# Gated mix of attention and a memory-recurrent transformer, forward and backward: crossbar transposes placed elsewhere in the forward recurrence, the value product's halves reordered, backward weights issued by GpSimd, sweep buffers allocated earlier

## The chip, the cores and the metric

The kernel runs on one core of one Trainium2 chip. The metric is the time of one execution on the device in microseconds, the median of several runs. The profile is taken from one execution of its own. The core's engines are PE (matrix products; PEld is its weight load), DVE (VectorE), ACT (ScalarE), POOL (GpSimd) and SP (SyncE). SP and POOL also issue DMAs, each in its own order: what stands behind a DMA that waits on such a queue waits too.

## The reference: what is computed

The output is a gated mix of two blocks over the same input x (2048 tokens, 576 columns, bf16), and the kernel returns it with the gradients of all inputs and weights:

```python
g = sigmoid((x * gate_w).sum(-1, keepdims=True))
a = A(x)      # 32 heads of 18 columns, one common k and v for all heads, softmax over all 2048 tokens
b = B(x)      # see below
return g * a + (1 - g) * b        # then vjp with grad_out

# B: 64 segments of 32 tokens, 32 heads of 128 columns, memory of 8 rows
mem = mem0
for s in range(64):
    h = concatenate([mem, x[32*s : 32*s+32]])           # 40 rows
    q, k, v = h @ Wq, h @ Wk, h @ Wv
    o = softmax(mask(q k^T * scale)) v @ Wo
    mem = o[:8];  outs.append(o[8:])
```

B is a chain: a segment's memory is the output of the one before, so its small products can't be batched over segments. A's work is large and free of order.

## The kernel before

**Stages.** From the trace: preparation and A's q and dO products (0 to 186 us), q, k and v of B for those tokens that need no place in the chain (`b_proj`, to 512), the forward weave (512 to 2372), the bulk of B's attention of the tokens (`b_bulk`, to 3112), the backward weave (to 4850), the backward of the tokens, the weight gradients and the end of A (to 6235).

**The weave.** `weave` runs two generators by turns. In the forward weave one is `b_chain_fwd`: 64 segments, each cut into 16 pieces by its `yield`s. The other is `a_pass1`, A's first sweep: 64 blocks of 512 rows, each of 16 steps. After each piece of the chain one step of the sweep follows, two steps ahead at the start. Thus a segment of the chain takes as long as one block of the sweep, and the order of the instructions is what the two generators write down. Engines run their own queues in that order.

**A sweep step** (`a_pass1`) makes the scores of the next key tile (a_S, PE), their exponent (a_E, ACT, L1459), the products dP (a_dP, PE), their product with the exponent (a_W, two DVE instructions, L1489), and adds both to an accumulator (a_acc, PE). At the end of a block `a_post` (L1519) turns the accumulator and stores three results (otok, dqtok, sd); it starts by a crossbar transpose of the block's query tile from DRAM (a_qt, L1523), and it runs in the steps with n % 16 in (1, 2, 5).

**A chain segment** (`b_chain_fwd`, L277) makes q, k and v rows of 32 tokens and memory in the layout of four column groups (`proj`, through `proj_part`; four matmuls for each of five row tiles of the input, each 512 columns wide). k comes in pieces 1 to 4, q in 4 to 8. `load_k` (L301) is a crossbar transpose of the segment's key rows; it is called in piece 11 for the next segment. `stash` (L314) is a crossbar transpose of 128 columns of a B weight, whose result `stash_end` stores as st_WT for the backward pass; two are done per segment in segments 0 to 47: the first is issued in piece 7 and stored in piece 14, the second issued in piece 14 and stored at the head of the next segment. The rows made are stored by POOL (`rows_out`) and copied on from DRAM to DRAM by SP (`rows_copy`, L343). In piece 10 the scores go into the bank px (64 columns of memory scores, 64 of token scores; in piece 11 64 columns of denominators follow, tile name c_x), then an exponent c_E (ACT, L425). In piece 11 the denominators are inverted (c_rd, DVE, L432) and the probabilities c_pn are made (L434).

The value product has two halves of 512 columns. v0 is made in pieces 9 to 11 in c_pj; v1 in two quarters of 256 columns (`proj_cols`): the first quarter in the free half of the scores' bank px in pieces 11 and 12, the second in c_pj in piece 12. Pieces 13 to 16 make the output o, its store and the 32 heads' product with Wo in many small matmuls (`heads`).

**The projections and the sweep's buffers.** `b_proj` ends with stores of its tokens' rows (L233). The sweep's buffers (KV, VK, WK by `load_A_kv`, L1403; the query tiles a_QD) lie in pools that are opened after b_proj's pools are closed.

**The backward weave** runs `b_chain_bwd` (L842) against `a_pass2` (L1564), A's second sweep. Its weights are loaded at its start: `load_WT` (L836) with six DMAs of 128 x 32 x 288 elements, all on SP; `load_WoT` (L550) with five DMAs, by turns on SP and POOL (`dq_eng`). The sweep's tiles b_QD (L1576) and b_SD (L1578) also come by SP's queue.

Of the kernel before, what the change touches and what calls it, by code (L numbers as in the profile page):

```python
# [11 lines left out]
BF16 = mybir.dt.bfloat16  # L12
F32 = mybir.dt.float32
P = 128

D = 576
NKT = 5
# [8 lines left out]
NPR = 16  # L26
# [13 lines left out]
class Kern:  # L40
# [169 lines left out]
    px = {}  # L210
# [47 lines left out]

    def proj_cols(self, out, st, Wt, lo, n, kts):
        for kt in kts:  # L260
            for c in range(4):
                self.mm(out[32 * c:32 * c + 32, :], lhsT=st[:, kt, :], rhs=Wt[:, kt, c * 1024 + lo:c * 1024 + lo + n],
                        start=(kt == 0), stop=(kt == NKT - 1), tp=(0, 32 * c))

    def proj_mem(self, st, Wt, j, psum, tag, nb):
# [10 lines left out]
    def b_chain_fwd(self, keep, sp, psum):  # L276
        nc = self.nc  # L277
# [39 lines left out]
        def stash_end(t, c):  # L317
            nc.sync.dma_start(self.st_WT[c // HB][:, c % HB, :], t[:])
# [5 lines left out]

        kx, vx = load_k(0), load_v(0)
        hs = hx = None
        for s in range(NSEG):
# [39 lines left out]

            if 0 < s <= 48:
                stash_end(*wt)
            if s:  # L370
# [11 lines left out]
            yield  # L382
            proj("k", 0, (0,), "c_pj")
            yield
            proj("k", 0, (1, 2, 3), "c_pj")
            yield
            proj("k", 0, (4,), "c_pj")
# [6 lines left out]
            rows_out("k")  # L394
            proj("q", 0, (1, 2), "c_pj")
            yield
            proj("q", 0, (3, 4), "c_pj")
            proj("q", 1, (0,), "c_x")
            if s < 48:
                wt = stash(2 * s)  # L400
            yield
            proj("q", 1, (1, 2, 3, 4), "c_x")
            rows_copy("k")
# [4 lines left out]
            rows_out("q")  # L408
            proj("v", 0, (0, 1), "c_pj")
            yield  # L410
            px = psum.tile([P, 512], F32, name="c_x", bufs=1)
            ps, den = px[:, 0:P], px[:, P:192]
# [12 lines left out]
            nc.scalar.activation(Et[:].rearrange("p a b -> p (a b)"), ps, ACT.Exp, scale=SCALEB)  # L425
            proj("v", 0, (2, 3), "c_pj")
            yield
            proj("v", 0, (4,), "c_pj")
            self.mm(den, lhsT=self.blockones[:], rhs=Et[:, 0, :], start=True, stop=False)
# [7 lines left out]
            nc.gpsimd.dma_start(self.pm_dram[s], pn[:].rearrange("p a b -> p (a b)"))  # L437
            if not last:
                kx = load_k(s + 1)
            vlo = px[:, 256:512]  # L440
            self.proj_cols(vlo, h_, self.W["v"], 512, 256, (0, 1, 2))
            yield
            self.proj_cols(vlo, h_, self.W["v"], 512, 256, (3, 4))
            nc.scalar.copy(t2["v"][:, 4:6, :].rearrange("p u e -> p (u e)"), vlo)
            pv = psum.tile([P, 512], F32, name="c_pj", bufs=1)
            self.proj_cols(pv[:, 0:256], h_, self.W["v"], 768, 256, range(NKT))
            nc.vector.tensor_copy(t2["v"][:, 6:8, :].rearrange("p u e -> p (u e)"), pv[:, 0:256])
            rows_copy("q")
# [14 lines left out]
            if not last:  # L463
                vx = load_v(s + 1)
                if s < 48:
                    stash_end(*wt)
                    wt = stash(2 * s + 1)
                ph = psum.tile([P, 512], F32, name="c_pj", bufs=1)
                heads(0, 11)
# [80 lines left out]
    def load_WoT(self, pool):  # L550
        self.WoT = pool.tile([P, NKT, J], BF16, name="WoT")
        self.nc.vector.memset(self.WoT[64:128, 4, :], 0.0)
        for kt in range(NKT):
            rows = KT_ROWS[kt]
            self.dq_eng().dma_start(self.WoT[0:rows, kt, :], self.st_WoT[kt][0:rows, :])

# [279 lines left out]
    def load_WT(self):  # L836
        for hf in range(2):
            c = slice(288 * hf, 288 * hf + 288)
            for wi in (2, 0, 1):
                self.nc.sync.dma_start(self.WT[wi][:, :, c], self.st_WT[wi][:, :, c])  # L840

# [561 lines left out]
    def load_A_kv(self, keep):  # L1403
        nc = self.nc
        self.KV = keep.tile([P, self.T], BF16, name="l_KV")
        nc.sync.dma_start(self.KV[:], self.kv_dram[:, :])
        self.VK = keep.tile([P, self.NTT, 64], BF16, name="l_VK")
        nc.sync.dma_start(self.VK[:], self.vk_dram[0])
        self.WK = keep.tile([P, self.NTT, 64], BF16, name="l_WK")
        nc.sync.dma_start(self.WK[:], self.vk_dram[1])  # L1410

    def a_qd_all(self, sp, psum):
# [24 lines left out]
    def a_pass1(self, keep, sp, psum, xps):  # L1437
# [3 lines left out]
        dl_all = keep.tile([P, NTT, NPR, 2, 2], BF16, name="a_dl")  # L1441
        QD, S, E_, W_ = {}, {}, {}, {}

        def load(b):
            if b < NB:
                p, qb = b // 4, b % 4
                QD[b] = sp.tile([P, 512], BF16, name="a_QD", bufs=3)
                nc.sync.dma_start(QD[b][:], self.qd_dram[p][:, qb * 512:(qb + 1) * 512])

# [16 lines left out]

        load(0)
        load(1)
        mm_S(0)
        ex(0)  # L1470
# [3 lines left out]
        for n in range(NP_ + 1):  # L1474
            if n < NP_:
                kt = n % 16
                if kt == 11:
                    load(n // 16 + 2)
                if n + 1 < NP_:
                    mm_S(n + 1)  # L1480
                dP = [psum.tile([P, 512], F32, name="a_dP", bufs=3) for _ in range(2)]
                for i in range(2):
                    r = slice(64 + 32 * i, 96 + 32 * i)
                    self.mm(dP[i][:], lhsT=self.KV[r, kt * P:kt * P + P], rhs=QD[n // 16][r, :], tp=(64 + 32 * i, 0))
                if n + 1 < NP_:
                    ex(n + 1)
                W_[n] = sp.tile([P, 2, 512], BF16, name="a_W", bufs=2)
                for i in range(2):
                    nc.vector.tensor_tensor(out=W_[n][:, i, :], in0=dP[i][:], in1=E_[n][:, i, :], op=ALU.mult)  # L1489
            if n > 0:  # L1490
                if n % 16 == 1:
                    acc = psum.tile([P, 512], F32, name="a_acc", bufs=1)
                    acc_mm(acc, n - 1, E_, self.VK, True, False)
                acc_mm(acc, n - 1, W_, self.WK, False, n % 16 == 0)
                if n % 16 == 0:
                    acs = sp.tile([P, 512], F32, name="a_acs", bufs=1)
                    nc.scalar.copy(acs[:], acc[:])
                    bb = n // 16 - 1
                    QD.pop(bb)
                    post = self.a_post(bb // 4, bb % 4, acs, sp, xps, dl_all)  # L1500
            if n < NP_ and n % 16:
                acc_mm(acc, n, E_, self.VK, False, False)
            if post is not None and n % 16 in (1, 2, 5):
                if next(post, "end") == "end":
                    post = None
            yield
# [12 lines left out]
    def a_post(self, p, qb, acs, sp, psum, dl_all):  # L1519
        nc = self.nc  # L1520
        dq_ = nc.gpsimd if (p, qb) == (NPR - 1, self.T // 512 - 1) else nc.sync
        qt = sp.tile([P, 4, 4, 32], BF16, name="a_qt", bufs=1)
        nc.sync.dma_start_transpose(qt[:].rearrange("p a b c -> p a (b c)"), self.qd_dram[p][:, qb * 512:(qb + 1) * 512])  # L1523
        pt = psum.tile([P, 4, P], F32, name="c_x", bufs=1)
# [6 lines left out]
        ptf = pt[:].rearrange("p a b -> p (a b)")  # L1531
        nc.scalar.copy(tkf, ptf)
        yield
        rl = sp.tile([P, 4, 2, 2], F32, name="a_rl", bufs=2)
# [203 lines left out]
def build_full(tc, A_x, A_wq, A_wk, A_wv, A_wo, B_mem0, B_Wq, B_Wk, B_Wv, B_Wo, gate_w, grad_out, outs_raw,  # L1738
# [9 lines left out]
    with SB("const") as cpool, tc.tile_pool(name="dram", bufs=1, space=bass.MemoryType.DRAM) as dram:  # L1748
# [14 lines left out]
        with ExitStack() as man:  # L1763
            man.enter_context(tc.manual_schedule())
            with SB("bwo") as bwo, SB("bw1") as bw1:
# [10 lines left out]
                with SB("bw2") as bw2:  # L1776
                    k.alloc_W(bw2, ("q",))
                    with SB("pxs") as pxs, PS("pxp") as pxp:
                        def extra(n):
                            if n == n0:  # L1780
                                for kt in range(NKT):
                                    k.load_W("q", kt)
                        k.b_proj(items, n0, len(items), pxs, pxp, extra)
                    with SB("a2k") as a2k, SB("cfs") as cfs, PS("cfp") as cfp, SB("a2s") as a2s, PS("a2p") as a2p:
                        k.load_A_kv(a2k)
                        k.weave(k.b_chain_fwd(a2k, cfs, cfp), k.a_pass1(a2k, a2s, a2p, cfp), 2)
            with SB("xw") as xw, SB("xl") as xl, SB("xs") as xs, PS("xp") as xp:
# [89 lines left out]
```

## Time and profile before

| | us |
|---|---|
| median of 3 runs | 6238.07 (6232.29 to 6254.74) |
| profiled execution | 6236.93 |
| its span in the trace | 6234.9 |
| forward weave, 512 to 2372 | 1860 |
| bulk of B's attention, 2372 to 3112 | 740 |
| backward weave, 3112 to 4850 | 1738 |
| PE busy | 5645.8 (91% of the span) |
| DVE busy | 3794.9 (61%) |
| ACT busy | 3389.5 (54%) |
| POOL busy | 1955.4 (31%) |

The profiled execution lies 1.1 us under the median. A row of the waits reads: engine, tile and line, then what released it, then the total of the waits in us, how many, and the longest. "issue" as a releaser means that the engine waited for nothing that the profile shows. SPq is SP's DMA queue.

### The profile page before, as it was taken

To read this page: it belongs to the slowest core of one execution; us is meant where nothing else is said; L and a number is where in the kernel's file an instruction comes from. 1 tells how busy PE (TensorE), PEld (TensorE's weight loads), DVE (VectorE), ACT (ScalarE), POOL (GpSimd) and SP (SyncE) were. 2 spreads that over 40 slices of the span, in tenths; PEclk is the share of its full clock that TensorE was granted. 3 is DMA by queue.
4 is the path that set the end of the run, shared out by engine and by line. 5 is a ranking of instruction groups with operands and counts; after the bars stand their busy time and mean duration, and the time that the engine had idled before them with its cause. 6 is when DMAs were issued, how large, how long until landed. Compare 5 with 4: busy or idle time off the path is not lost.

```text
span 6234.9 us, 214080 instructions
## 1 busy us (share of the span) xinstructions
PE 5645.8 (91%) x91339; PEld 3294.1 (53%) x91550; DVE 3794.9 (61%) x7192; ACT 3389.5 (54%) x4852; POOL 1955.4 (31%) x3481
## 2 busy tenths in 40 slices
PE   6898999999999998999859999999999899899998
PEld 4443444444444445777725555555555687675444
DVE  4335877777787886666558888888887111111112
ACT  3325777777777775656547777777776222211101
POOL 3002333333333334444413333333333211112213
PEclk9999999999999999999969999999999899999999
DMA  4645666666666548999864344443434899896653
GB/s 144 217 154 118 129 128 121 126 123 130 128 129 118 114 98 224 255 255 251 249 176 108 108 108 108 109 110 109 110 110 102 212 250 251 232 278 202 219 184 110
DMA packets 1426721, 998.59 MB, mean 160 GB/s; under 512 B 965597, under 2 KB 1245030, under 8 KB 1415814
## 3 DMA queue, kind: packets, MB, share of 16 engines
q1 hardware_dynamic: 1344294, 790.82, 52.0%
q0 software_dynamic: 81472, 194.07, 9.9%
q8 instruction: 717, 11.75, 0.8%
q14 instruction: 238, 1.95, 0.1%
HBM read 550.31 MB, written 385.03 MB: 150 GB/s over the span
## 4 chain that ended last, share of the span: by engine, by line
PE 34%; ACT 11%; issue 9%; DMA 5%; SPq 2%; POOL 2%; DVE 0%; POOLq 0%; DVEq 0%; ACTq 0%
ACT b_E L1597 10%; PE w_acc L75 10%; PE b_S L75 6%; PE r_pj L75 4%; PE r_x L75 3%; DMA dsx_dram<-x_dS 3%; PE x_tr L80 2%; PE b_acc L75 2%; PE x_po L75 1%; PE x_b L75 1%; PE x_m L75 1%; PE f_big L75 1%; PE b_dP L75 1%; PE x_S L75 1%; SPq L840 1%
## 5 line engine op out<-in xcount | busy, mean ns | idle before, releaser
L1489 DVE TENSOR_TENSOR a_W<-a_dP,a_E 128x512 bf16<-128x512 f32 x2048 | 1318.4, 686 | 357.1 <-issue 135.7
L1618 DVE TENSOR_TENSOR b_dS<-b_dP,b_E 128x512 bf16<-128x512 f32 x2048 | 1312.9, 683 | 268.5 <-issue 149.6
L1459 ACT ACTIVATE a_E<-a_S 128x1024 bf16<-128x1024 f32 x1024 | 1048.2, 1024 | 472.1 <-PE a_dP L75 229.1
L1597 ACT ACTIVATE b_E<-b_S 128x1024 bf16<-128x1024 f32 x1024 | 1047.8, 1023 | 457.3 <-PE b_dP L75 358.5
L75 PE MATMUL b_S<-b_KV,b_QD 32*128 32x512 bf16 x2048 | 406.2, 386 | 192.7 <-ACT b_E L1597 117.8
L75 PE MATMUL r_pj<-WT,r_dT 128*32 128x288 bf16 x12288 | 493.6, 288 | 1.1 <-ACT r_hs L950 1.1
L75 PE MATMUL w_acc<-w_d,w_h 128*128 128x512 bf16 (+1 forms) x2352 | 470.9, 379 | 2.5
L75 PE MATMUL a_S<-a_QD,l_KV 32*128 32x512 bf16 x2048 | 402.2, 386 | 27.8 <-ACT a_E L1459 10.4
L75 PE MATMUL b_acc<-b_dS,b_SD 128*32 128x512 bf16 x2048 | 424.2, 396 | 1.5 <-DMA b_SD<-sd_dram 1.2
L75 PE MATMUL a_acc<-a_W,l_WK 128*32 128x512 bf16 x4096 | 417.5, 393 | 1.6 <-issue 1.3
L75 PE MATMUL a_acc<-a_E,l_VK 128*32 128x512 bf16 x4096 | 409.7, 384 | 6.6 <-issue 2.7
L75 PE MATMUL b_acc<-b_E,b_SD 128*32 128x512 bf16 x2048 | 409.0, 396 | 0.0
L75 PE MATMUL b_dP<-b_KV,b_QD 32*128 32x512 bf16 x2048 | 404.7, 391 | 1.3 <-DVE b_dS L1618 1.3
L75 PE MATMUL a_dP<-a_QD,l_KV 32*128 32x512 bf16 x2048 | 401.9, 388 | 3.5 <-issue 3.5
L75 PEld LDWEIGHTS <-r_dT 128*32 128x32 bf16 x12288 | 333.7, 97 | 80.4 <-issue 2.0
L1084 DVE COPY y_T<-y_pt 128x512 bf16<-128x512 bf16 x256 | 96.8, 419 | 451.1 <-PE y_pt L80 433.7
L75 PEld LDWEIGHTS <-b_QD 32*128 32x128 bf16 x4096 | 165.6, 91 | 389.1 <-issue 315.1
L75 PEld LDWEIGHTS <-w_h 128*128 128x128 bf16 (+1 forms) x2688 | 229.8, 100 | 258.4 <-issue 6.6
L75 PEld LDWEIGHTS <-hm 128*32 128x32 bf16 x8960 | 226.6, 97 | 238.1 <-issue 79.6
L75 PEld LDWEIGHTS <-l_KV 32*128 32x128 bf16 x4096 | 119.3, 91 | 321.0 <-issue 288.9
L1070 ACT CAST y_tdk<-y_pk 128x512 bf16<-128x512 f32 x128 | 75.0, 586 | 377.7 <-PE y_pk L75 213.4
L75 PE MATMUL y_pdx<-WT,y_T 128*128 128x288 bf16 x2048 | 271.8, 286 | 0.0
(422 smaller groups left out, 11253.6 us busy)
## 6 DMA issues: line engine op xcount, KB each, us to landing
b_QD<-qd_dram SPq DMA_DIRECT2D x256, 128.0 KB
b_SD<-sd_dram SPq DMA_DIRECT2D x256, 128.0 KB
dOx_dram<-p_tok SPq DMA_DIRECT2D x16, 1024.0 KB
c_vx<-vx_dram SPq DMA_DIRECT2D x256, 64.0 KB
krow_dram<-c_k POOLq DMA_DIRECT2D x64, 256.0 KB, 3.1
qrow_dram<-c_q POOLq DMA_DIRECT2D x64, 256.0 KB, 3.6
vrow_dram<-c_v POOLq DMA_DIRECT2D x64, 256.0 KB, 5.4
x_q<-qx_dram SPq DMA_DIRECT2D x32, 512.0 KB
```

What stands on the lines that cost most here:

```text
L75: return self.nc.tensor.matmul(out, lhsT, rhs, start=start, stop=stop, tile_position=tp, skip_group_check=True)
L80: return self.nc.tensor.transpose(out, in_, self.identB[b:b + nrows, b:b + nrows], tile_position=tp)
L840: self.nc.sync.dma_start(self.WT[wi][:, :, c], self.st_WT[wi][:, :, c])
L1070: nc.scalar.copy(d[w][:, r, :], pk[:])
L1084: nc.vector.tensor_copy(T_[t][w][:], pt[:])
L1459: nc.scalar.activation(E_[n][:], S.pop(n)[:], ACT.Exp, scale=SCALEA)
L1489: nc.vector.tensor_tensor(out=W_[n][:, i, :], in0=dP[i][:], in1=E_[n][:, i, :], op=ALU.mult)
L1597: nc.scalar.activation(E_[n][:], S.pop(n)[:], ACT.Exp, scale=SCALEA)
L1618: nc.vector.tensor_tensor(out=D_[n][:, i, :], in0=dP[i][:], in1=E_[n][:, i, :], op=ALU.mult)
```

## The change

It has four parts.

1. The order of the crossbar transposes in the forward weave. `load_k(s)` is called in piece 2 of the segment that uses it. `a_post` has one more `yield` and transposes a_qt after it, and runs in the steps (1, 2, 3, 6). `stash` is called in pieces 3 and 6, `stash_end` in 6 and 9.
2. The value product. v0 is made in pieces 8 to 10 and copied out in halves by ACT and DVE; v1 is made in c_pj in full width of 512 in pieces 11 and 12. px holds the scores and denominators alone. `proj_cols` is gone. One group of q's second half comes a piece earlier.
3. The DMAs of `load_WT` and `load_WoT` are all issued by GpSimd's queue.
4. The sweep's buffers and query tiles lie in a pool that is opened before the last projections, and their loads are issued four items before the end of those.

```diff
 # b_chain_fwd
-        kx, vx = load_k(0), load_v(0)
+        vx = load_v(0)
...
-            if 0 < s <= 48:
-                stash_end(*wt)
...
             proj("k", 0, (0,), "c_pj")
+            kx = load_k(s)
             yield
             proj("k", 0, (1, 2, 3), "c_pj")
+            if s < 48:
+                wt = stash(2 * s)
...
             proj("q", 0, (1, 2), "c_pj")
+            if s < 48:
+                stash_end(*wt)
+                wt = stash(2 * s + 1)
             yield
             proj("q", 0, (3, 4), "c_pj")
-            proj("q", 1, (0,), "c_x")
-            if s < 48:
-                wt = stash(2 * s)
-            yield
-            proj("q", 1, (1, 2, 3, 4), "c_x")
+            proj("q", 1, (0, 1), "c_x")
+            yield
+            proj("q", 1, (2, 3, 4), "c_x")
+            proj("v", 0, (0,), "c_pj")
             rows_copy("k")
...
-            proj("v", 0, (0, 1), "c_pj")
-            yield
-            px = psum.tile([P, 512], F32, name="c_x", bufs=1)
+            proj("v", 0, (1, 2), "c_pj")
+            if s < 48:
+                stash_end(*wt)
+            yield
+            px = psum.tile([P, 192], F32, name="c_x", bufs=1)
...
-            proj("v", 0, (2, 3), "c_pj")
-            yield
-            proj("v", 0, (4,), "c_pj")
+            self.proj_part(pj["v", 0], h_, self.W["v"], 0, (3, 4))
+            nc.scalar.copy(t2["v"][:, 0:2, :].rearrange("p u e -> p (u e)"), pj["v", 0][:, 0:256])
+            nc.vector.tensor_copy(t2["v"][:, 2:4, :].rearrange("p u e -> p (u e)"), pj["v", 0][:, 256:512])
+            yield
...
-            if not last:
-                kx = load_k(s + 1)
-            vlo = px[:, 256:512]
-            self.proj_cols(vlo, h_, self.W["v"], 512, 256, (0, 1, 2))
-            yield
-            self.proj_cols(vlo, h_, self.W["v"], 512, 256, (3, 4))
-            nc.scalar.copy(t2["v"][:, 4:6, :].rearrange("p u e -> p (u e)"), vlo)
-            pv = psum.tile([P, 512], F32, name="c_pj", bufs=1)
-            self.proj_cols(pv[:, 0:256], h_, self.W["v"], 768, 256, range(NKT))
-            nc.vector.tensor_copy(t2["v"][:, 6:8, :].rearrange("p u e -> p (u e)"), pv[:, 0:256])
+            proj("v", 1, (0, 1), "c_pj")
+            yield
+            proj("v", 1, (2, 3, 4), "c_pj")
             rows_copy("q")
...
                 vx = load_v(s + 1)
-                if s < 48:
-                    stash_end(*wt)
-                    wt = stash(2 * s + 1)
 # load_WoT
-            self.dq_eng().dma_start(self.WoT[0:rows, kt, :], self.st_WoT[kt][0:rows, :])
+            self.nc.gpsimd.dma_start(self.WoT[0:rows, kt, :], self.st_WoT[kt][0:rows, :])
 # load_WT
-                self.nc.sync.dma_start(self.WT[wi][:, :, c], self.st_WT[wi][:, :, c])
+                self.nc.gpsimd.dma_start(self.WT[wi][:, :, c], self.st_WT[wi][:, :, c])
 # load_A_kv (the same function load, with load(0) and load(1), is gone from a_pass1)
+                self.QD[b] = keep.tile([P, 512], BF16, name="a_QD", bufs=3)
+                nc.sync.dma_start(self.QD[b][:], self.qd_dram[p][:, qb * 512:(qb + 1) * 512])
...
+        load(0)
+        load(1)
 # a_pass1
-            if post is not None and n % 16 in (1, 2, 5):
+            if post is not None and n % 16 in (1, 2, 3, 6):
 # a_post
-        qt = sp.tile([P, 4, 4, 32], BF16, name="a_qt", bufs=1)
-        nc.sync.dma_start_transpose(qt[:].rearrange("p a b c -> p a (b c)"), self.qd_dram[p][:, qb * 512:(qb + 1) * 512])
...
         nc.scalar.copy(tkf, ptf)
+        yield
+        qt = sp.tile([P, 4, 4, 32], BF16, name="a_qt", bufs=1)
+        nc.sync.dma_start_transpose(qt[:].rearrange("p a b c -> p a (b c)"), self.qd_dram[p][:, qb * 512:(qb + 1) * 512])
         yield
 # build_full
+                    with SB("a2k") as a2k:
+                        with SB("pxs") as pxs, PS("pxp") as pxp:
...
+                                elif n == len(items) - 4:
+                                    k.load_A_kv(a2k)
-                    with SB("a2k") as a2k, SB("cfs") as cfs, PS("cfp") as cfp, SB("a2s") as a2s, PS("a2p") as a2p:
-                        k.load_A_kv(a2k)
-                        k.weave(k.b_chain_fwd(a2k, cfs, cfp), k.a_pass1(a2k, a2s, a2p, cfp), 2)
+                        with SB("cfs") as cfs, PS("cfp") as cfp, SB("a2s") as a2s, PS("a2p") as a2p:
+                            k.weave(k.b_chain_fwd(a2k, cfs, cfp), k.a_pass1(a2k, a2s, a2p, cfp), 2)
```

More of the change, by code (lines that the diff above doesn't have):

```diff
@@ L257, in proj_part @@
                         start=(kt == 0), stop=(kt == NKT - 1), tp=(0, 32 * c))
[L259 to L263, printed above, removed]
     def proj_mem(self, st, Wt, j, psum, tag, nb):
@@ L1410, in load_A_kv, with load @@
         nc.sync.dma_start(self.WK[:], self.vk_dram[1])
+        self.QD = {}
+        def load(b):
+            if b < NPR * (self.T // 512):
+                p, qb = b // 4, b % 4
+                self.QD[b] = keep.tile([P, 512], BF16, name="a_QD", bufs=3)
+                nc.sync.dma_start(self.QD[b][:], self.qd_dram[p][:, qb * 512:(qb + 1) * 512])
+        self.load_QD = load
+        load(0)
+        load(1)
     def a_qd_all(self, sp, psum):
@@ L1441, in a_pass1 @@
         dl_all = keep.tile([P, NTT, NPR, 2, 2], BF16, name="a_dl")
[L1442 to L1448, printed above, removed]
+        S, E_, W_ = {}, {}, {}
+        QD, load = self.QD, self.load_QD
         def mm_S(n):
@@ L1465, in acc_mm @@
                         rhs=t[:, g // 2, :], start=first, stop=last, tp=(0, 32 * g))
-        load(0)
-        load(1)
         mm_S(0)
@@ L1777, in build_full, with extra @@
                     k.alloc_W(bw2, ("q",))
[L1778 to L1783, printed above, removed]
-                    with SB("a2k") as a2k, SB("cfs") as cfs, PS("cfp") as cfp, SB("a2s") as a2s, PS("a2p") as a2p:
-                        k.load_A_kv(a2k)
-                        k.weave(k.b_chain_fwd(a2k, cfs, cfp), k.a_pass1(a2k, a2s, a2p, cfp), 2)
+                    with SB("a2k") as a2k:
+                        with SB("pxs") as pxs, PS("pxp") as pxp:
+                            def extra(n):
+                                if n == n0:
+                                    for kt in range(NKT):
+                                        k.load_W("q", kt)
+                                elif n == len(items) - 4:
+                                    k.load_A_kv(a2k)
+                            k.b_proj(items, n0, len(items), pxs, pxp, extra)
+                        with SB("cfs") as cfs, PS("cfp") as cfp, SB("a2s") as a2s, PS("a2p") as a2p:
+                            k.weave(k.b_chain_fwd(a2k, cfs, cfp), k.a_pass1(a2k, a2s, a2p, cfp), 2)
             with SB("xw") as xw, SB("xl") as xl, SB("xs") as xs, PS("xp") as xp:
```

## The prediction

> **What bounds the kernel now.** I read the page first, then the stages, the waits of each stage, and the timeline around the longest. The page has PE busy for 91% of the span, but it also gives DVE 61% and ACT 54%, so the loss must be looked for by stage. The row of the forward weave (stretch, length, then busy PE, PEld, DVE, ACT, POOL, granted clock, DMA share, GB/s):
>
> ```profile
> 516.00:2371.00 1855.00, 1710.48 (x36718) 782.15 (x36711) 1467.84 (x2683) 1339.18 (x1724) 692.99 (x1406) 0.99 0.63 121
> ```
>
> PE is busy 92% at full clock, so 144.5 us are idle there. The waits of that stretch (total, how many, longest):
>
> ```profile
> DVE a_W L1489 <- issue: 135.7, 313, 5.3
> ACT a_E L1459 <- issue: 102.1, 72, 4.6
> PE c_x L75 <- DVE c_rd L432: 65.4, 64, 2.2
> PE c_pj L75 <- issue: 26.5, 23, 4.1
> ```
>
> Two kinds of loss stand here. One is a true wait, once in each of the 64 segments: PE waits 1.02 us for the reciprocal c_rd. The other is "issue": an engine stands still though nothing visible holds it. The timeline of one segment shows both (start, duration, engine, operation, wait in brackets):
>
> ```profile
> 1502.27 1.22 SPq L1523 DMA_TRANSPOSE a_qt<-qd_dram  x1
> ...
> 1508.84 0.41 PE L75 MATMUL c_x<-c_qT,c_kmT 128*8 128x8 bf16 x30
> 1510.12 0.17 PE L75 MATMUL c_x<-c_qT,c_kmT 128*8 128x8 bf16 x2 [0.88 <-issue]
> 1511.20 1.29 DVE L1489 TENSOR_TENSOR a_W<-a_dP,a_E 128x512 bf16<-128x512 f32 x2 [1.58 <-ACT c_E L425]
> 1511.77 0.23 PE L75 MATMUL c_x<-c_E,blockones 128*128 128x64 bf16 x2
> 1512.41 0.55 DVE L432 RECIPROCAL c_rd<-c_x 128x64 f32<-128x64 f32 x1
> 1513.01 0.51 PE L75 MATMUL c_x<-Wv,hm 128*32 128x256 bf16 x12 [1.00 <-DVE c_rd L432]
> ```
>
> c_rd reads the bank into which PE wants to write the value product, so PE waits until it is done. And the score products, many small instructions, stop for 0.88 us soon after a crossbar transpose was issued.
>
> I tested the second kind over the whole stage. The first a_S products of successive steps give each piece's length; the medians of pieces 1 to 16 sum to 27.41 us. The mean segment is 29.24 in segments 1 to 47, which also transpose two weight columns each, and 28.00 after. Put against the transposes' flights (DMA records of 256-byte reads): outside pieces 2 to 9, 146 pieces with a transpose in flight for over half their length exceed the median by 0.29 us, 110 partly covered by 0.23, 120 without by 0.09. In pieces 2 to 9, which hold wide products (few instructions per us), the excess is 0.02 with or without. In the later segments, narrow pieces show 0.23 with a flight and 0.03 without. So the loss sits where a transpose meets many small instructions.
>
> At the stage's start and in the backward weave:
>
> ```profile
> 506.34 0.33 SPq L1406 DMA_DIRECT2D l_KV<-kv_dram  x1
> 511.82 0.61 PE L75 MATMUL a_S<-a_QD,l_KV 32*128 32x512 bf16 x2 [10.13 <-DMA a_QD<-qd_dram]
> ```
> ```profile
> 3147.86 37.30 SPq L840 DMA_DIRECT2D WT<-st_WT  x6
> 3185.26 7.04 SPq L1576 DMA_DIRECT2D b_QD<-qd_dram  x1
> ```
> ```profile
> PE b_S L75 <- DMA b_QD<-qd_dram: 48.2, 2, 40.2
> ```
>
> SP's queue issues six weight loads for 37.30 us, and the sweep's tile b_QD stands behind them: PE waits 40.2 us once (the other 8 are the stage's start). Between 3155 and 3195 PE is busy 0.90 us.
>
> **Part 1: transposes moved.** Per segment SP issues the same DMAs in another order: a_qt, the keys and both weight columns now stand at pieces 2, 3 and 6 and their stores at 6 and 9, before the row copies that they followed. Adding SP's issue times, I place three of the four flights in pieces 4 to 8 and the second weight column in 12 to 13. In segments 1 to 47 the narrow excess is 146 x 0.29 + 110 x 0.23 + 120 x 0.09 = 78.4 us. At the 0.03 of the later segments without a flight, 376 narrow pieces would keep 11, so 67 go; 27 later ones give 27 x 0.20 = 5. That is the best case, 72. The second column stays in narrow pieces, 48 x 0.3 = 15: I take **−57**. The least, with 0.09 as the floor: 146 x 0.20 + 110 x 0.14 = 45, less 20 if the second column's flight spreads: −25.
> The price could be on SP. It now issues for 20.3 us per segment and waits 9.0; the two waits for the weight columns' landings are 2.8 each (146.9 us in 52). 20.3 + 2 x 2.8 = 25.9 us fits under PE's segment of some 27.5. The keys, formerly fetched a segment ahead, are now issued at about 7 us and land 5.2 later, at some 12; piece 10 wants them at about 14. That cover is 2 us.
>
> The Trainium skill speaks against this term: its page "Runtime: NRT & Kernel Launch", section "Instruction fetch mechanics", says that instructions are streamed in 16 KiB blocks by DMA and that crossing a block is mostly hidden. If the "issue" stops are such fetches and are hidden, this part is worth nothing and the sum is that of the first rival below; the row of 0.29 against 0.09 us decides for me that they are not hidden while transposes fly.
>
> **Part 2: value halves.** The second half no longer uses the scores' bank: as 512-wide products it waits for c_rd no more, 65.4 us. Per segment 20 matmuls and 20 weight loads go; the streamed columns stay. What is late next is DVE. Around piece 11 it must do a_W (1.29 for two), c_rd 0.55 and c_pn 0.29 in one piece, 2.13 us, where PE's piece with two groups takes 0.92 + 2 x 0.21 plus 0.23 for the denominators, 1.58; the step after then waits for a_W. So piece 11 goes from a median 2.77 to about 2.13, and piece 7, with one more group, pays 0.2 at most: −0.5 per segment, x 64 = **−30**. Bounds: −65 if DVE catches up for nothing, −10 if the halved value copy, now on DVE and ACT between the same steps, delays them by another 0.3 us (two copies of 256 columns).
>
> **Part 3: sweep buffers apart.** The KV load is issued four items earlier in the projections. PE's last product ends at 501.69 and it waits 10.13 at 511.82. The order of the changed program still lets the first exponent wait for the projections' last stores (issued 502.33, landed about 506): −6 (between −4 and −9.5).
>
> **Part 4: backward weights by GpSimd.** SP is free of the 37.30 us, so b_QD no longer waits: up to 40.2 + 2.3 (a wait for another weight, WoT) + a few us behind = −46. The loads (2304 KB each) now run on POOL after its dmT store at about 3149. Behind them on POOL are the next dO-memory tiles, the expansions and the products' weights. At the pace of the SP issue (6.2 us each), or 7.4, all six have landed by 3193; the chain's first product wants its half at about 3172, when two have. POOL's own issue cost per DMA, from its rows:
>
> ```profile
> 523.86 1.18 POOL L296 DMA_DIRECT2D otok_dram<-zeros  x1
> 2394.79 1.85 POOL L199 DMA_DIRECT2D WoN<-in_B_Wo_dram  x2
> ```
>
> That is 1.18 for 2048 rows and 0.92 for 1024, so some 2 us for the 4096 rows of a WT load (estimate). WoT's 4.5 MB wholly on POOL gain 2.3 and may delay a later tile by as much. I take **−40**. If each load took 12 us, POOL would hold PE for some 18 to 20 of the 40: the bound −20.
>
> The same skill also has a rule here: "DMA: Bandwidth & Descriptors", section "Issuing engines are not separate DMA queues", says that another issuing engine saves only the sequencer's issue time, usually small beside the transfer. By it this term would be about nothing; the rows show 37.30 us of issue on SP with b_QD's issue right behind, so here it is not small.
>
> **Sum** against the profiled execution's 6236.93: −57 − 30 − 6 − 40 = −133, 6104. The median of the runs is 6238.07, 1.1 more: **6105**.
>
> **Rivals.** (a) The issue stops are not the transposes'. For it: ACT a_E and DVE a_W wait for "issue" in all segments, and 0.09 remains without a flight. Against: 0.23 to 0.29 with. Then −76 remains: 6162. (b) GpSimd's loads are slow, at 12 us each: −113, 6125. For it: nothing of this size goes over that queue in this stage now. (c) SP becomes the bound. If its 25.9 us rise to 28.5 (one more landing wait of 2.6), segments 0 to 47 gain 29.24 − 28.5 = 0.74 each, 35 in all; with 40 + 6 and 8 from the last 16 segments that is −89: 6149. (d) DVE does not limit: the full 65 gives −168: 6070. (e) **Slower**: SP falls into a row of landing waits. Its queue is in order, and each transposition's store waits for the transposition, with key rows and value loads behind. The gains elsewhere (40 + 6 + 8 = 54) over 48 segments are 1.1 us, so it decides from 29.24 + 1.1 = 30.4 us per segment. At 31.5 (20.3 + 9.0, and 2.2 of the row copies' mean wait once more) it costs 48 x 2.26 = 108, less 54: 6292. (f) It does less than it says: at 30 us per segment, 37 lost and 54 won, −17: 6221.
>
> **Chances.** Forecast (6080 to 6115) 0.44; (a) 0.19; (b) 0.10; (c) 0.08; (d) 0.07; (f) 0.06; (e) 0.06. The range leaves out (e) and (f), 0.12. Every part at its best gives −72 − 65 − 9.5 − 46 = −192, 6044; every part at its least −25 − 10 − 4 − 20 = −59, 6178, and (a) with a small loss besides 6190. As all bests together are unlikely I take 6050 to 6190. Half a per cent, about what a measurement of this kernel can tell, is 31 us: faster 0.88 (forecast, (a) to (d)), same 0.06 (f), slower 0.06 (e).
>
> **What would show it.** In the forward stretch, PE's wait for c_rd is gone and instead a_acc waits for a_W, about 0.5 us in piece 11; "issue" waits of ACT and DVE fall by half; the segment is near 27.5 us; SP has idle time. In the backward stretch no PE wait over some 5 us stands before 3200 on the old scale, and the WT loads take under 8 us each on POOL. Wrong would be: a mean segment over 28.5, PE waiting for c_kx or for the rows read back, or a new wait for WT or for dO tiles of tens of us.

## The result and the profile after

| | before | after |
|---|---|---|
| median of 4 runs, us | 6237.45 | 6149.73 (6139.97 to 6154.94) |
| span of the profiled execution | 6234.9 | 6138.2 |
| first steady sweep step begins at | 515.3 | 507.8 |
| forward weave (that step to the last a_S) | 1853.0 | 1782.6 |
| segments 1 to 47, each | 29.24 | 28.02 |
| segments 48 to 62, each | 28.00 | 27.14 |
| backward weave (first b_S to last r_x) | 1733.1 | 1714.4 |

The ratio is 0.9853 (95% interval 0.983 to 0.9876): 88 us faster, not the 133 of the forecast, and within its range. The profiled execution was the fastest of the four; the forward weave of the same code also ran at 1795.7 in another profile, so single profiles of this version differ by some 13 us. The other stages, whose code is the same, differ by up to 8 us between the profiles (from the last a_S to the first b_S, 741.3 to 748.8 us in those of before, after and e1 to e8).

The row of the forward weave after (columns as before):

```profile
512.00:2294.00 1782.00, 1730.01 (x35416) 743.35 (x35416) 1456.94 (x2677) 1356.35 (x1723) 692.99 (x1405) 0.99 0.64 126
```

PE is idle for 52 us of it, where it was 144.5. What PE still waits for there:

```profile
PE c_x L75 <- DMA c_kx<-kx_dram: 30.3, 23, 2.9
PE c_pj L75 <- DMA hm<-in_B_mem_dram: 5.4, 3, 4.1
PE c_pj L75 <- issue: 2.5, 5, 1.3
```

c_rd is gone from this list, and the "issue" stops of c_pj fell from 26.5 to 2.5. Of the "issue" waits of other engines that the prediction wanted halved, ACT's a_E fell from 102.1 to 1.3 us, DVE's a_W only from 135.7 to 89.7. New is c_kx: PE waits for the key transposition in 23 segments. SP's queue in one segment says why (start, duration):

```profile
1444.26 0.61 SPq L329 DMA_DIRECT2D oh_dram<-c_oh  x1
1444.97 4.35 SPq L337 DMA_DIRECT2D vm_dram<-vrow_dram  x1
1449.37 0.60 SPq L339 DMA_DIRECT2D vx_dram<-vrow_dram  x1
1450.03 0.46 SPq L287 DMA_DIRECT2D hm<-xT_dram  x1
1450.53 2.73 SPq L295 DMA_TRANSPOSE c_kx<-kx_dram  x1
```

vm copies 32 rows, as km and qm do in 0.6 us, yet its issue holds SP for 4.35 us; the keys stand behind it. Over segments 1 to 47 the keys are issued at a median of 10.1 us of the segment and their last read starts at 15.2; piece 10, which uses them, starts at 15.07. (By the count in which the keys are called in piece 2, k's products lie in pieces 2 to 5 and q's in 5 to 8.)

A late key costs more than the wait. After eight of the ten waits for c_kx that are longer than 1.5 us, and after none of the 13 shorter ones, the granted TensorE clock is 0.50 for 3.4 us; a_dP's matmuls then take 0.60 us, where their median is 0.38. One of these stretches (columns as before, the clock behind POOL):

```profile
1459.10:1462.40 3.30, 3.30 (x31) 0.67 (x26) 3.00 (x7) 1.68 (x2) 2.34 (x5) 0.50 0.63 225
```

There are eight such stretches in this stage, 27 us in all, as there are eight of 34 us in the kernel before.

What bounds pieces 11 to 13 now is DVE. Its timeline shows it working from the value copy to c_oT with a gap of 0.21 us:

```profile
1429.10 0.42 DVE L427 CAST c_v<-c_pj 128x256 bf16<-128x256 f32 x1 [0.77 <-ACT c_v L426]
1429.44 1.28 DVE L1483 TENSOR_TENSOR a_W<-a_dP,a_E 128x512 bf16<-128x512 f32 x2
1430.64 0.55 DVE L432 RECIPROCAL c_rd<-c_x 128x64 f32<-128x64 f32 x1
1431.27 0.29 DVE L434 TENSOR_TENSOR c_pn<-c_E,c_rd 128x128 bf16<-128x128 bf16 x1
1431.48 2.48 DVE L1483 TENSOR_TENSOR a_W<-a_dP,a_E 128x512 bf16<-128x512 f32 x4
1434.17 0.42 DVE L450 CAST c_oT<-c_pj 128x256 bf16<-128x256 f32 x1 [0.21 <-PE c_pj L75]
```

In the backward weave, the PE wait of 40.2 us is gone, but two of a quarter of it stand in its place (PE timeline, wait in brackets), and GpSimd stands still for three of its WT loads:

```profile
3098.39 0.18 PE L75 MATMUL r_x<-r_dSB,r_kx 128*128 128x32 bf16 x1 [11.66 <-POOL r_dSB L236]
3122.34 0.60 PE L75 MATMUL b_S<-b_KV,b_QD 32*128 32x512 bf16 x2 [10.34 <-DMA b_QD<-qd_dram]
```
```profile
3063.89 5.05 POOL L830 DMA_DIRECT2D WT<-st_WT  x3
3077.46 1.69 POOL L830 DMA_DIRECT2D WT<-st_WT  x1 [8.52 <-issue]
3085.49 1.68 POOL L830 DMA_DIRECT2D WT<-st_WT  x1 [6.33 <-issue]
3093.50 1.68 POOL L830 DMA_DIRECT2D WT<-st_WT  x1 [6.33 <-issue]
3095.17 2.07 POOL L903 DMA_DIRECT2D dOm_dram<-r_dOm  x4
3097.26 1.08 POOL L236 TENSOR_TENSOR r_dSB<-r_dS,bmask 128x512 bf16<-128x512 bf16 x1
```

### The profile page after: what moved, and what is told of

The parts are those of the page before. It is cut to its first block, busy times and chain, and to the rows that moved or that the text cites. A ratio compares the mean times of both kernels' runs of the same rounds, so it can differ in the third digit from the quotient of the medians.

```text
span 6138.2 us, 211534 instructions
## 1 busy us (share of the span) xinstructions
PE 5684.2 (93%) x90270; PEld 3256.7 (53%) x90270; DVE 3786.6 (62%) x7192; ACT 3410.6 (56%) x4852; POOL 1968.7 (32%) x3490
## 5 line engine op out<-in xcount | busy, mean ns | idle before, releaser
L75 PE MATMUL a_acc<-a_W,l_WK 128*32 128x512 bf16 x4096 | 446.1, 392 | 0.2 <-DVE a_W L1483 0.2
L75 PE MATMUL a_acc<-a_E,l_VK 128*32 128x512 bf16 x4096 | 429.0, 384 | 4.4
L75 PE MATMUL a_dP<-a_QD,l_KV 32*128 32x512 bf16 x2048 | 414.3, 387 | 0.2 <-DVE a_W L1483 0.2
L75 PEld LDWEIGHTS <-hm 128*32 128x32 bf16 x7680 | 192.0, 96 | 171.5 <-DVE a_W L1483 10.4
```

The source lines that it names most:

```text
L75: return self.nc.tensor.matmul(out, lhsT, rhs, start=start, stop=stop, tile_position=tp, skip_group_check=True)
```

## The experiments

Three questions were open: why the keys are late, why the backward gained half of what was forecast, and whether transposes in flight beside many small instructions are what stops PE. Each ratio is to the kernel before on the same chip.

| run | median us | ratio (95%) | forward weave | backward weave |
|---|---|---|---|---|
| the change | 6149.73 | 0.9853 (0.983 to 0.9876) | 1782.6 | 1714.4 |
| e1 WT in two parts | 6138.73 | 0.9838 (0.9824 to 0.9853) | 1795.7 | 1708.2 |
| e2 keys first | 6148.31 | 0.9858 (0.9841 to 0.9874) | 1778.0 | 1714.1 |
| e3 oh by GpSimd | 6109.76 | 0.9792 (0.9777 to 0.9806) | 1747.2 | 1710.5 |
| e4 value copy by ACT | 6139.54 | 0.9834 (0.9819 to 0.9849) | 1789.0 | 1710.9 |
| e5 old places | 6199.53 | 0.9925 (0.9906 to 0.9945) | 1829.9 | 1713.5 |
| e6 plain loads (before) | 6234.67 | 0.9984 (0.9974 to 0.9993) | 1850.0 | 1732.8 |
| e7 WT whole | 6153.63 | 0.9855 (0.9839 to 0.9872) | 1783.2 | 1712.5 |
| e8 e3 + e4 + e7 | 6097.98 | 0.9764 (0.975 to 0.9779) | 1744.2 | 1713.1 |
| e9 e3 and extra transposes | 6168.06 | 0.9888 (0.9838 to 0.9937) | 1813.5 | 1711.7 |
| e10 e3 and extra plain loads | 6149.00 | 0.9857 (0.9804 to 0.991) | 1790.8 | 1713.2 |
| e11 e8 + e2 | 6112.24 | 0.9801 (0.976 to 0.9843) | 1756.2 | 1710.0 |
| e12 e8, keys at old place | 6163.04 | 0.9763 (0.9738 to 0.9789) | 1801.1 | 1709.5 |

e12 ran on a chip on which the kernel before took 6315.21, so only its ratio compares. The two stage columns are from one profile each.

**e3 and e2: why the keys are late.**

```diff
-                nc.sync.dma_start(self.oh_dram[s // 16][:, :, c0:c0 + 8], ...)
+                nc.gpsimd.dma_start(self.oh_dram[s // 16][:, :, c0:c0 + 8], ...)
```

> The changed kernel, with the store oh (4096 pieces of 16 bytes) issued by GpSimd instead of SP. Theory 1: vm's 4.26 us of issue on SP are the backlog of those pieces in the queue; then vm's issue falls to under 1 us, the keys are issued some 4 us earlier, c_kx's wait goes and segments 1 to 47 fall to about 27.3 us, the whole by some 35 to about 6115. Rival: vm's issue time is its own or that of the value loads ahead of it; then it stays above 3 us, and the segment at about 28.

vm's issue fell to 0.60 us, segments 1 to 47 to 27.30, the forward weave by 35.4. The waits of PE in that stage, and the wait of SP ahead of the keys:

```profile
PE c_pj L75 <- DMA hm<-in_B_mem_dram: 6.1, 3, 4.1
PE c_x L75 <- DMA c_kx<-kx_dram: 5.0, 9, 1.3
```
```profile
SPq L295 <- DMA qx_dram<-qrow_dram: 170.5, 47, 5.9
```

So the theory holds in its cause: the 16-byte pieces of oh, issued on SP ahead, held SP. It does not hold in its path. The keys are issued no earlier at the median (9.8 us, where 4 us earlier was forecast): SP now waits some 4 us between the hm load and the keys (in the program each DMA waits for the one eight places ahead of it, here a copy of q rows; 170.5 us in 47 segments). But their last read starts at 13.9 instead of 15.2. With the longest wait for c_kx at 1.3 us, no stretch at half clock is left in this stage.

```diff
             kx = load_k(s)
+            if pend:
+                pend("v")        # rows_copy("v") of the segment before
...
-            rows_copy("v")
+            pend = rows_copy
```

> The changed kernel, with the copy of a segment's value rows (vm, vx) moved on SP behind the next segment's key transposition. Theory 1: the keys are late because the transposition stands behind vm's 4.26 us of issue; then the keys are issued at about 5 us of the segment instead of 10, PE's wait for c_kx (30.3 us in 23) goes, segments 1 to 47 fall from 28.02 to about 27.3 us and the whole by some 35 to about 6115. Rival: SP's lap is the limit; then another wait takes its place (value rows, the query tile or the stores), and the segment stays within 0.2 us of 28.0.

The stall moved to whatever stood behind oh: hm's issue now took 4.31 us. c_kx's wait fell to 8.8 us, but c_PB came with 13.8 in its place (all 13 times behind GpSimd's product with a_qt, which had waited for a_qt to land), and the segment only to 27.89. That was the rival. It also shows that the backlog belongs to oh and not to vm.

**e1 and e7: the backward weights.**

```diff
             nc.gpsimd.memset(t[:], 0.0)
+        self.load_WT((0,))        # first half here; the second half at the old place
```

> The changed kernel, with the three WT loads of the first half issued on GpSimd's queue right after its memsets at the start of the backward weave, the three of the second half where all six stood. Theory 1: the backward weave gained 19 us and not 40 because the six loads fill GpSimd's queue (8.5, 6.3 and 6.3 us of standing still), so r_dSB behind them came 11.7 us late and a b_QD 10.3 us late after it. Then both waits go: the weave (first b_S to last r_x) falls from 1714 to about 1694 us and the whole to about 6130. Rival: the transfers themselves are the limit (some 24 us from issue to landing); then PE waits for WT in place of r_dSB, 15 us or more, and the weave stays at about 1714.

The weave fell by 2 to 6 us against runs of the same code (1710.5 to 1714.4), not by 20. GpSimd no longer stood still between its WT loads, but the chain's first loads on SP now met the weights: r_pT was issued at 3074 and landed at 3090, GpSimd and DVE waited for it, and PE waited 14.3 us for DVE:

```profile
PE b_dP L75 <- DVE b_dS L1614: 14.3, 1, 14.3
PE b_S L75 <- DMA b_QD<-qd_dram: 12.3, 4, 8.2
```

The first theory falls; the rival's core holds, with the wait in another place.

```diff
-        for hf in range(2):
-            c = slice(288 * hf, 288 * hf + 288)
-            for wi in (2, 0, 1):
-                self.nc.gpsimd.dma_start(self.WT[wi][:, :, c], self.st_WT[wi][:, :, c])
+        for wi in (2, 0, 1):
+            self.nc.gpsimd.dma_start(self.WT[wi][:].rearrange("p h d -> p (h d)"),
+                                     self.st_WT[wi][:, :, :].rearrange("p h d -> p (h d)"))
```

> The changed kernel, with WT loaded by three DMAs of whole rows (36,864 bytes on end per partition) in place of six of 576-byte pieces, at the same place on GpSimd's queue. Theory 1: the six loads are limited by the engines' time for small pieces (DMA share 1.00 at 300 GB/s over 50 us) and by GpSimd standing still 21 us for room; with long pieces GpSimd issues in under 1 us each, r_dSB is on time, and the 13.8 MB pass in less than 46 us; then the waits of 11.7 and 10.3 us go, the backward weave falls from 1714 (1710 to 1714 in the runs of the same code) to about 1692 us and the whole by 20 to about 6130. Rival: the bytes are the limit; then the third load lands no earlier than 46 us after the first issue, PE waits for WT some 10 us instead, and the weave stays above 1705.

GpSimd issues each in 0.65 us and r_dSB is on time, but the three loads take 26.9, 32.3 and 37.7 us to land, and the sweep's tiles come late beside them (b_QD 24.1 us in 5, b_SD 8.4 in 2): 1712.5. The theory's rate came (all landed some 38 us after the first issue, not 46), the rival's wait for WT did not, and still the weave stayed above the rival's 1705. The engines' share and rate in these stretches, the kernel before (weights on SP), the change, and e7, one row each:

```profile
3155.00:3195.00 40.00, 0.90 (x8) 0.29 (x7) 2.02 (x4) 1.26 (x2) 0.27 (x1) 0.55 1.12 325
```
```profile
3064.00:3096.00 32.00, 15.96 (x205) 5.73 (x202) 19.03 (x32) 15.00 (x17) 10.82 (x9) 0.60 0.97 302
```
```profile
3068.00:3108.00 40.00, 15.15 (x212) 5.33 (x204) 18.32 (x32) 14.67 (x17) 6.17 (x10) 0.61 0.98 380
```

The DMA share is about 1 in all three: 14.2 MB (six loads of 128 x 32 x 288 elements of 2 bytes; the expectation's 13.8 is a slip) at 300 GB/s are 47 us, at 380 still 37. Another issuing queue lets PE work beside the transfer (15 to 16 us busy of some 32 to 40, against 0.9) but doesn't make it shorter, and each order tried makes something else late for 22 to 33 us (11.66 + 10.34 after the change, 14.3 + 12.3 in e1, 24.1 + 8.4 in e7).

**e4: DVE in pieces 11 to 13.**

```diff
-            nc.scalar.copy(t2["v"][:, 0:2, :]..., pj["v", 0][:, 0:256])
-            nc.vector.tensor_copy(t2["v"][:, 2:4, :]..., pj["v", 0][:, 256:512])
+            nc.scalar.copy(flat(t2["v"], 0), pj["v", 0][:])
```

> The changed kernel, with the first value half copied out by ACT alone (one copy of 512 columns instead of 256 on each of ACT and DVE). Theory 1: in pieces 11 to 13 DVE is the limit (it works without a gap from the value copy to c_oT in the trace); without its 0.42 us copy, piece 13 falls from 2.09 to some 1.7 us: -0.3 to -0.4 per segment, 64 segments, about -22, the whole to about 6128. Rival: PE waits there for c_PB or ACT; then pieces 10 to 13 together change by under 0.1 us, or grow as ACT is now 0.2 us later for its exponent.

The medians of pieces 11 to 13 went from 1.58, 1.79, 2.09 to 1.67, 1.55, 1.93: −0.31, and the undisturbed segments 48 to 62 from 27.14 to 26.98. In these segments, pieces 10 to 13 together fell from 7.39 to 7.13. So DVE was the limit there. Over all segments the median of piece 10 rose by 0.24, as the keys were later still (50.4 us); with it the four pieces changed by 0.08 only, which is the rival's figure, and the gain is hidden in this profile.

**e5 and e6: are the transposes the cause?**

> The changed kernel, with the crossbar transposes (keys, query tile, weight columns) at the places of the kernel before; value halves, backward queue and buffers stay changed. Theory 1: transposes in flight beside the narrow pieces cost what the prediction said; then the narrow pieces of segments 1 to 47 are above their medians by about 1.7 us per segment again, and the segment is about 27.05 + 1.8 = 28.85 us, 0.8 over the changed kernel with its late keys and 1.5 over the version without late keys (27.30). Rival: the transposes' places matter nothing, and the gain came from elsewhere; then, as the keys are no longer late, the segment is at about 27.3 us, and the whole near 6110.

The edit puts `load_k`, `stash`, `stash_end` and the a_qt transpose back to their lines of the kernel before. The run measures the transposes' places alone: 45 us by the ratios (0.9925 to 0.9853), 47 by the forward weave (1829.9 to 1782.6). The segment came to 28.91: theory 1's 28.85. But that the number fits is partly luck, for the waits are mostly not stops:

```profile
PE c_pj L75 <- POOL c_PB L236: 23.0, 32, 4.0
PE c_pj L75 <- DVE c_v L423: 8.2, 17, 1.5
PE c_pj L75 <- issue: 7.9, 11, 1.7
```

The largest is an order on GpSimd: all 32 times its product with a_qt stands ahead of c_PB and has waited for a_qt to land.

```diff
 # kernel before, stash
-            nc.sync.dma_start_transpose(t[:].rearrange("p (o d) -> p o d", o=1), src[:, E * h:E * h + E])
+            nc.sync.dma_start(t[:, 0:512].rearrange("p (k e) -> p k e", k=4),
+                              src[0:512, E * h:E * h + E].rearrange("(k p) e -> p k e", p=P))
+            nc.sync.dma_start(t[:, 512:576], src[448:576, E * h:E * h + 64])
```

> The kernel before, with the two weight-column transposes of a segment replaced by plain loads of the same weight in 256-byte and 128-byte pieces at the same places on the same queue; the backward weights are then not transposed, so that the gradients through them are another computation of the same size. Theory 1: the crossbar's flight is what stops the narrow pieces; then segments 1 to 47 fall from 29.24 towards the 28.0 of those without weight columns, by 1.0 to 1.2 us each, and the whole by 47 to 56 us to about 6187. Rival: any DMA of that size on the queue does it (or SP's time); then the segment stays at 29.0 to 29.3 and the whole within 10 us of 6241.

29.24 became 29.08, 0.16 of the 1.0 to 1.2 that theory 1 asked for; segments 48 to 62, the same code in both, differ by as much (28.00 and 28.22). So for the weight columns the crossbar is not the cause: plain loads at their places leave the loss as it was, and that is the rival. Whether the loads or SP's order make it, this run doesn't say.

I then counted PE's stops, its "issue" waits of over 0.5 us in the forward weave. There are 30 of 36.3 us together in the kernel before, 26 of 30.6 in e6, 11 of 12.2 in e5, 2 of 1.8 after the change, 1 of 0.5 in e3, none in e8. So most of them went without the transposes' new places: from 36.3 to 12.2 us with the other parts of the change (e5), from 12.2 to 1.8 with the places, by one profile each. Which other part did it was not tried. The trace also has the DMA records of PE's instruction blocks (the queue kind "instruction", 288 blocks of 16,384 bytes in that stage for some 73,400 PE and PEld records, so one per 255). In the kernel before 17 of the 30 stops, 22.3 us, end 1.2 to 1.6 us after such a block has ended; by chance it would be 6 in 100. This suggests that a good part of the stops is PE waiting for its instructions; no run changes that alone. The blocks' own transfer is not what grows: 1.15 us at the median with a transpose in flight, 1.08 without. The Trainium skill, page "Runtime: NRT & Kernel Launch", section "Instruction fetch mechanics", calls the crossing of a block mostly hidden: the trace agrees for most blocks, even in the kernel before, where 17 of 288 have such a stop behind them, against 1 of 278 in e3.

**e8: the three edits together.** From independent gains about 6080 was expected, or 6092 with ACT as the limit; it came to 6098. WT in whole rows gave nothing again (1713.1). The value copy gave 0.26 us per segment in segments 48 to 62 (27.11 in e3, 26.85), but nothing in 1 to 47 (27.30 in both), as PE's wait for c_kx rose from 5.0 to 17.0 us.

**e9 to e12: which flight.**

```diff
 # e3, segments 48 to 62; e10 with a plain load of 512 pieces of 256 bytes instead
                 vx = load_v(s + 1)
+                for j in range(3 if s >= 48 else 0):
+                    stash(s + j)
```

> The version with oh on GpSimd (segments 48 to 62 there: 27.11 us, per-piece excess over the medians near nothing), with three additional crossbar transposes of a weight column in each of the segments 48 to 62, issued one after the other behind the value loads, so that they fly beside the narrow pieces 14 to 16 and the first pieces after them; what they bring is not used. Theory 1 (the crossbar's flight stops narrow pieces): pieces 14 to 16, 1 and 11 of these segments exceed their medians by 0.4 to 0.8 us per segment more than before. Theory 2 (any load in flight there does it): the same. Rival (neither; it was SP's order): under 0.1 us.

> As the run with three additional transposes, but with three plain loads of 512 pieces of 256 bytes of the same weight at the same places. Theory 1 (the crossbar's flight): under 0.1 us per segment. Theory 2 (any load in flight delays PE's instruction blocks, in the way that the plain loads in the kernel before left 29.08 of 29.24 us): 0.4 to 0.8 us, like the transposes. Rival (neither): under 0.1 in both runs.

Neither theory's 0.4 to 0.8 us came. Segments 48 to 62 went from 27.11 to 30.92 (e9) and 29.43 (e10), but pieces 14 to 16 and 1 to 9 stayed within 0.08 us of e3. Nearly all of it stands in piece 10 and the next: 1.85 became 5.19 and 3.82, c_kx's wait alone 44.8 and 26.8 us. The extra loads held SP, and SP's lateness arrived at PE as late keys. The test is narrower than it was meant to be: the three loads of a segment write one buffer and were issued 4 to 10 us apart, so that most flew beside the wide pieces 2 to 9. Of the narrow pieces 14 to 16 and 1, a flight covers more than half in only 9 (e9) and 10 (e10); their excess is -0.01 and 0.01 us. The second weight column of the change itself covers more than half of 29 pieces 14 and 15, at an excess of 0.01.

> The version with the three edits (oh by GpSimd, value half by ACT, WT whole; 6098), with the copy of the value rows also moved behind the next key transposition. Its remaining wait for c_kx is 17 us in the profile. Theory 1: with hm and the keys ahead of vm the keys are issued 1 to 2 us earlier and piece 10 goes from a mean 2.30 to under 2.0: -0.3 x 47 = -14, about 6084. Rival: the keys wait for the landing of the DMA eight places earlier, whatever stands between; then c_kx's wait stays above 12 us or c_vx's takes its place, and the whole stays within 6 us of 6098.

The keys were issued 6 us earlier than in e8 (at 5.0, not 10.9) and c_kx's wait fell to 4.6 us, against the rival; but c_PB's came with 10.6, and the whole was not faster than e8, against theory 1. As in e2, GpSimd's product with a late a_qt stands ahead of c_PB each time.

```diff
 # e8
-            kx = load_k(s)           # piece 2
...
+            if not last:             # piece 11
+                kx = load_k(s + 1)
```

> The version with the three edits (6098; segments 1 to 47 at 27.30 us, of which 0.45 are late keys in piece 10, and PE's stops for no visible cause nearly gone), with the key transposition alone put back into piece 11 of the segment before, so that on SP it is issued at some 25 us of the segment and flies beside the narrow pieces 15, 16 and 1. Theory 1 (the key transposition's flight stops PE's instructions there): pieces 15, 16 and 1 exceed their medians by 0.5 to 0.9 us per segment, as in the kernel before (0.91), c_kx's wait goes; the segment is at 27.4 to 27.8 and the whole at 6100 to 6120. Rival (what counted was SP's order and a late query tile, not the flight): these pieces exceed by under 0.15 us, the segment falls to 26.9 to 27.0 and the whole to about 6080.

The wait for c_kx went, and the ratio is that of e8. The two largest waits of PE:

```profile
PE c_pj L75 <- POOL c_PB L236: 25.7, 16, 3.9
PE c_pj L75 <- issue: 8.7, 12, 2.5
```

c_PB waits behind a late a_qt again. The "issue" stops of over 0.5 us are 9 of 10.9 us, where e8 has none, so something of the transposition's flight shows. But pieces 15, 16 and 1, which the expectation names, exceed their medians by 0.13 us in segments 1 to 47, the rival's figure, and by 0.36 in 48 to 62, between the two. (There the keys fly earlier, and pieces 14, 15 and 16 exceed by 0.25, 0.21 and 0.17; 0.00, 0.04 and 0.01 in e8.) So it is likely, and not shown, that the key transposition stops narrow pieces: this was another, slower chip, on which e8 has no profile, and the DMA engines were busy for 0.75 of the stage at 124 GB/s, in e8 for 0.65 at 128. The query tile's place was never changed alone.

## Why the prediction was right, and where not

The direction, the place of each gain and the range were right; −133 was 45 too much. By its steps:

- **Part 1, −57.** It gave about −49: 1853.0 to 1782.6 is −70, less some 21 of Part 2; e5 has −47 for the places alone. Without late keys (e3) it would have been more than forecast: 1853.0 to 1747.2 is −106, less 21, so −85 with oh moved too. What failed is the sentence "That cover is 2 us": the keys were issued at 10.1, not 7, and their last read began at 15.2, where they were to land at 12. I had added up SP's issue times with vm's at its old cost (2.17 in the kernel before), where oh was issued later in the segment; it became 4.26. That cost 35 us, and with it came a sign that the prediction had listed as one of being wrong, PE waiting for c_kx.
- **Its reason** was half right. The stops went, as forecast (36.3 to 1.8 us), but only 10.4 of the 34.5 us are shown for the transposes' places (e5); there the larger cost of the old places is the order on GpSimd behind a_qt, 23.0 us. I pooled all transposes in flight (0.29 against 0.09 us), and such a correlation doesn't tell a flight from what comes with it: the weight columns show no excess in e9 and after the change, the key transposition may (e12). That the excess was small in wide pieces held in every trace but e12's (0.05 us per piece, at most 0.03 elsewhere).
- **Part 2, −30.** Medians: piece 7 +0.19, piece 11 −1.19, piece 12 +0.15, piece 13 +0.52; −0.33 by 64 is −21 (e5 against the kernel before has −23). DVE was indeed late next, as e4 shows, but its cost fell on piece 13: it pays where DVE's backlog meets c_oT, not where it begins. I left the value copy's 0.42 us out of the taken value.
- **Part 3, −6.** Measured 515.3 to 507.8, of which 1.4 was already there at the end of the projections: −6.1. The reason held too: the first exponent waits 4.08 us for the projections' last store.
- **Part 4, −40.** Measured −19, just under the least that was allowed. The mis-sized term is the cover "all six have landed by 3193": the loads took about 8 us each, GpSimd stood still for 21 us, and r_dSB and then a b_QD came late (11.66 and 10.34 us, where "no PE wait over some 5 us" was to be seen). My bound of −20 was tied to 12 us a load; it was reached at 8, since r_dSB waits behind the last issue. The rule of the Trainium skill ("DMA: Bandwidth & Descriptors", section "Issuing engines are not separate DMA queues") that another issuing engine saves only the time of the issue was nearer than I allowed: e1 and e7 show that the bytes remain, and the change saved 19 of the 40 us, about what PE could work beside them (16 us of 32).
- **Rival (c)**, SP as the bound, came closest in mechanism: SP's order cost PE time, at 28.02 us per segment where (c) had 28.5. That its sum, 6149, is the measured time is luck: it held the full 40 of Part 4, and a landing wait where an issue was slow. The forecast itself (6080 to 6115) didn't come.

What stays open: by what PE's instructions come late, if that is what the stops are, when the blocks' transfers take no longer; what in the change's other parts removed two thirds of the stops; and what the flights of the keys and of the query tile cost by themselves.

## What to carry to other kernels

Before moving a DMA on an in-order queue, find what stands ahead of it at its new place and what that costs there: here a store of 4096 tiny pieces charged whichever DMA came next. When a large load moves to another queue, compare its bytes by the rate at a DMA share of 1 with the time in which the compute can do without it; only the rest can be gained. And a correlation of stalls with "a transfer in flight" should be split by kind of transfer before it is priced.

## What the runs showed of the hardware that was not expected

- The store oh (128 x 32 pieces of 16 bytes) issues in 0.6 us on SP, but the DMA behind it takes 4.3 us to issue, be it vm (4.26) or hm (4.31). From GpSimd it costs 1.67 us of issue, and the DMA behind it on SP 0.60.
- In the stretches with loads of 576-byte pieces 293 to 328 GB/s passed at a DMA share of 0.97 to 1.12, from either queue; with pieces of 36,864 bytes it was 380 GB/s at 0.98. GpSimd takes three loads of 4096 pieces and then stands still for 6.3 to 8.5 us before each next.
- PE's "issue" stops of over 0.5 us in one stage went from 36.3 us to 0.5 (e3) while its matmuls in that stage only fell from 36,718 to 35,414.
- After PE's waits for c_kx of over 1.5 us the granted clock was 0.50 for 3.4 us in eight of ten cases, so a late key was paid for a second time.
